# Two heads of a pair in one key tile and one query tile, in the first batch of a decay attention

## The chip, the cores and the metric

The kernel runs on one core of a Trainium2 chip. The metric is the device time of one execution in microseconds (us). A core has TensorE (PE; its weight loads are listed as PEld), VectorE (DVE), ScalarE (ACT), GpSimd (POOL) and SyncE (SP), which issues the DMAs. Each engine works through its own instructions in their order and waits on the others by semaphores.

## The reference

Causal attention with a decay, for 4 batches, 8 heads, 576 tokens and a head dimension of 64, followed by two feed-forward layers over 2304 tokens (width 512, inner width 2048):

```python
scores = scale * np.matmul(q, k.transpose(0, 1, 3, 2))
cum = np.cumsum(np.log(np.clip(f, 0.0001, 1.0)), axis=-1)
scores = np.where(causal, -1e9, scores + cum[..., :, None] - cum[..., None, :])
attn = softmax(scores)                 # over keys
x = (attn @ v), heads side by side     # 2304 x 512
h = x @ w_in;  g = max(h, 0) + alpha * min(h, 0);  x = g @ w_out     # layer 1
h = x @ w2_in; g = h where h >= 1, 0 where h <= -1, else (h + 1)**2 / 4;  out = g @ w2_out   # layer 2
```

All inputs and weights of the layers come as 64-bit words; q, k, v and f are float32 in the kernel.

## The kernel before

Numbers that need more than the short float32 format of TensorE (float32r) are split in two: a high part, which is the value cast to float32r (ScalarE), and a low part, which is the value less its high part (VectorE). A product of two such numbers is then a sum of products of parts.

**Attention.** The loop `for u, pr in head_list()` (line 446) goes over 8 units and 4 pairs of heads in each. A unit is a batch and a range of queries: 0 to 256, or 256 to 576. Units 0 and 1 are batch 0; the code calls them `plain` (line 451). They lie before the phase in which values and probabilities are split too, so their product with the values runs in plain float32 (line 714), while later batches use three float32r products (lines 720 to 722).

For each pair of heads: k and q of both heads are loaded (`load_k`, `load_q`, lines 465 and 469), keys with both heads side by side (128 columns, 64 of each head), queries with room for two copies of each head. `dup_q` (line 478, ScalarE) fills the second copy. TensorE transposes the keys in chunks of at most 512 columns (`ktr`, line 499): rows 0 to 63 of the result are head 0, rows 64 to 127 head 1. From it each head gets a key tile of its own (`khi` and `klo`, lines 512 and 515): the high part in the 64 rows of that head, the low part in the other 64. A head's query tiles (`qtr`, `qhi`, `qlo`, lines 528 to 540) hold the same query twice, over all 128 rows, as high part and as low part. The scores of a block of 128 keys are then two products over 128 rows (`qk`, line 602): key tile with the query's high part, and with its low part:

```python
for t in range(2):
    nc.tensor.matmul(out=sb.t[:, :m], lhsT=kt.t[:, kb * P:(kb + 1) * P],
                     rhs=qt.t[t][:, qo:qo + m], start=(t == 0), stop=(t == 1))
```

A head of unit 0 has 2 blocks (256 and 128 queries), one of unit 1 has 5 (320, 320, 320, 192 and 64). Each block goes from PSUM to SBUF with its bias (ScalarE, line 618), its diagonal part is masked by GpSimd (line 442), VectorE takes the maximum over blocks (lines 637 and 655), GpSimd the maximum over partitions (line 661, `Mb`), VectorE subtracts (line 677), ScalarE takes the exponential (line 680), TensorE multiplies with the values (line 714). Two columns of sums are inverted and spread over the partitions by DMAs (lines 764 to 778), and the result is split into the layer's input (lines 794 and 797).

**Layers.** The 32 pieces of layer 1's weights are converted from 64-bit words while batch 0's attention runs (`convert`, line 816): one ScalarE instruction, four on VectorE (lines 843 to 862), then the high part (line 870) and the low part (line 875). A piece may start once the piece two before it is done. Layer 1 runs over 9 chunks of 256 tokens and 16 slices of the inner width each (`l1_slice`, line 911: `ps_h`, line 922, and `ps_y`, line 961); chunk 0's slice s needs pieces 2s and 2s + 1. All slices are in one fixed order. Layer 2 follows (lines 1097 and 1144).

**Order of the work.** Nothing is emitted in the order of the loops. `Order.emit` (line 113) simulates the engines with durations written in the code (`pe`, `dve`, `act`, lines 257 to 270) and latencies (`LAT`), and at each step gives an engine that is free the ready task of lowest position. Batch 0's attention has positions from -60 to -36, the conversions from -9 up, the slices from about -2 up: attention goes first and conversions fill what is left. Buffers come from rings (line 297): 2 for queries (`q`), 2 for key tiles (`k`), 3 PSUM banks for transposes and scores (`s`), one query load buffer and in batch 0 a second one (`qr`, `qr1`). SP's queue holds all DMAs in the planned order; a load that waits for its buffer holds up what is behind it.

Of the kernel before, what the change touches and what calls it, by code (L numbers as in the profile page):

```python
# [10 lines left out]
F32 = mybir.dt.float32  # L11
# [4 lines left out]
ALU = mybir.AluOpType  # L16
# [84 lines left out]
class Order:  # L101
# [6 lines left out]
    def add(self, eng, dur, fn, pos, deps=(), new=(), use=(), share=1.0, move=0):  # L108
        t = Task(eng, dur, fn, pos, deps, list(new), list(use), share, move)
        self.tasks.append(t)  # L110
        return t
# [81 lines left out]
def kernel(  # L193
# [63 lines left out]
    def pe(n, cnt=1):  # L257
        return cnt * (max(n, 240) / 2.4 + 13)
# [4 lines left out]
    def dve(n, ptr=False):  # L263
        return 68 + n * 1.042 + (60 if ptr else 0)
# [4 lines left out]
    def act(n, bias=False):  # L269
        return 93 + n * 0.833 + (93 if bias else 0)  # L270
# [68 lines left out]

    KC = 4 * P


# [29 lines left out]
    for t in RAW:  # L374
        nc.gpsimd.memset(t[S % P:, NKB - 1], 0.0)
    for t in QR:
        nc.gpsimd.memset(t[S % P:, 2], 0.0)

    first = cpool.tile([P, 2], F32, name="first")
    nc.gpsimd.partition_all_reduce(first, ident[:, :2], P, ReduceOp.max)  # L380
# [1 line left out]
    def load_tok(dst, src, b, pr, t0, t1):  # L382
        n = (t1 - t0) // P
        for j in range(2):
            if n:
                nc.sync.dma_start(
                    out=dst[:, 0:n, j, :],
                    in_=src[b, 2 * pr + j, t0:t0 + n * P, :].rearrange("(c p) d -> p c d", p=P))
        r = t1 - t0 - n * P
        if r:  # L390
            nc.sync.dma_start(
                out=dst[:r, n, :, :],
                in_=src[b, 2 * pr:2 * pr + 2, t0 + n * P:t1, :].rearrange("h p d -> p h d"))
# [52 lines left out]
    for u, pr in head_list():  # L446
# [19 lines left out]
            kb_.t = RAW[kb_.slot]  # L466
            load_tok(kb_.t, k, b, pr, 0, nk)

        def load_q(qb_=qb_, b=b, pr=pr, q0=q0, q1=q1):
            qb_.t = QR[0] if qb_.ring is R["qr"] else ph["qr"]  # L470
            load_tok(qb_.t[:, :, :, 0, :], q, b, pr, q0, q1)

        T["lk"] = add("SP", tok_issue(0, nk), load_k, p0 - 3, [last.get("lv"), last.get("lk")], new=[kb_],
                      move=moved(2 * nk, 256))
# [4 lines left out]
            t = qb_.t[:, :-(-n // P)]  # L479
            nc.scalar.copy(out=t[:, :, :, 1, :], in_=t[:, :, :, 0, :])  # L480

        T["lq"] = add("ACT", act(-(-n // P) * P), dup_q, p0 - 2, [last["lq"]], use=[qb_])


        nsplit = sum(y[2] > PVF for y in blocks)
# [8 lines left out]

        for t0 in range(0, nkp, KC):
            t1 = min(nkp, t0 + KC)
            pb = Buf(R["s"])

            def ktr(pb=pb, kb_=kb_, t0=t0, t1=t1):
                pb.t = ps_a.tile([P, 512], F32, tag=f"s{pb.slot}", name="pst")  # L500
                for c in range(t0 // P, t1 // P):
                    nc.tensor.transpose(
                        pb.t[:, c * P - t0:(c + 1) * P - t0],
                        kb_.t[:, c, :, :].rearrange("p j d -> p (j d)"), ident)

            a = last["ktr"] = add("PE", 112 * (t1 - t0) // P, ktr, p0 - 1, [T["lk"], last.get("ktr")],
                                  new=[pb] + (kx if t0 == 0 else []), use=[kb_] + ([] if t0 == 0 else kx))
            for j in range(2):
                hr = slice(j * D, (j + 1) * D)
                lr = slice(D - j * D, 2 * D - j * D)  # L510

                def khi(j=j, hr=hr, pb=pb, t0=t0, t1=t1, k_of=k_of):
                    nc.scalar.copy(out=k_of(j)[hr, t0:t1], in_=pb.t[hr, :t1 - t0])

                def klo(j=j, hr=hr, lr=lr, pb=pb, t0=t0, t1=t1, k_of=k_of):
                    nc.vector.tensor_tensor(out=k_of(j)[lr, t0:t1], in0=pb.t[hr, :t1 - t0],  # L516
                                            in1=k_of(j)[hr, t0:t1].bitcast(F32), op=ALU.subtract)

                h = add("ACT", act(t1 - t0), khi, p0 - 1, [a], use=[pb, kx[j]])
                kready[j] += [h, add("DVE", dve(t1 - t0), klo, p0 - 1, [h], use=[pb, kx[j]])]  # L520

        qx, qready = [], [[], []]
        for j in range(2):
            pb, qb = Buf(R["s"]), Buf(R["q"])
            qx.append(qb)
            np_ = -(-n // P)

            def qtr(pb=pb, qb_=qb_, j=j, np_=np_):
                pb.t = ps_a.tile([P, 512], F32, tag=f"s{pb.slot}", name="pst")
                for c in range(np_):  # L530
                    nc.tensor.transpose(  # L531
                        pb.t[:, c * P:(c + 1) * P], qb_.t[:, c, j].rearrange("p x d -> p (x d)"), ident)

            def qhi(pb=pb, qb=qb, n=n):
                qb.t = [ap1.tile([P, NMAX], F32R, tag=f"q{x}{qb.slot}", name=f"q{x}") for x in "HL"]
                nc.scalar.copy(out=qb.t[0][:, :n], in_=pb.t[:, :n])

            def qlo(pb=pb, qb=qb, n=n):
                nc.vector.tensor_tensor(out=qb.t[1][:, :n], in0=pb.t[:, :n], in1=qb.t[0][:, :n].bitcast(F32),
                                        op=ALU.subtract)  # L540

            a = add("PE", 112 * np_, qtr, pos_of(2 * pr + j) - 1, [T["lq"], last.get("qtr")], new=[pb], use=[qb_])
            last["qtr"] = a
            h = add("ACT", act(n), qhi, pos_of(2 * pr + j) - 1, [a], new=[qb], use=[pb])
            qready[j] = [h, add("DVE", dve(n), qlo, pos_of(2 * pr + j) - 1, [h], use=[pb, qb])]
# [36 lines left out]
        for j in range(2):  # L582
# [16 lines left out]
            for x, (kb, qo, m, off) in enumerate(blocks):  # L599
                sb = Buf(R["s"])  # L600

                def qk(sb=sb, kb=kb, qo=qo, m=m, kt=kx[j], qt=qx[j]):
                    sb.t = ps_a.tile([P, 512], F32, tag=f"s{sb.slot}", name="ps_s")
                    for t in range(2):
                        nc.tensor.matmul(out=sb.t[:, :m], lhsT=kt.t[:, kb * P:(kb + 1) * P],  # L605
                                         rhs=qt.t[t][:, qo:qo + m], start=(t == 0), stop=(t == 1))

                a = add("PE", pe(m, 2), qk, pb_, kready[j] + qready[j] + [last_qk], new=[sb], use=[qx[j], kx[j]],
                        share=min(1.0, m / 256))
                last_qk = a  # L610
                sbufs.append((sb, a))

                Sb, so, new = S_of[kb]

                def evac(Sb=Sb, sb=sb, m=m, so=so, new=new, bias=nb[:, kb, hd:hd + 1]):
                    if new:
                        Sb.t = ap2.tile([P, GMAX], F32, tag=f"S{Sb.slot}", name="S")
                    nc.scalar.activation(out=Sb.t[:, so:so + m], in_=sb.t[:, :m], func=AF.Identity, bias=bias)  # L618

                e = last["ev"] = add("ACT", act(m, True) - 30, evac, pb_, [a, nb_ready, last.get("ev")], new=[Sb] if new else [],  # L620
                                     use=[sb] + ([] if new else [Sb]))
                base = q0 + qo - kb * P
                w = min(m, P - base)
                if w > 0:
                    e = add("POOL", 300, lambda Sb=Sb, so=so, w=w, base=base: causal(
                        Sb.t[:, so:so + w], base), pb_, [e], use=[Sb])
                ev.append(e)
# [587 lines left out]
```

## Time and profile before

| | us |
|---|---|
| median of 3 runs | 1079.76 (1079.24 to 1083.73) |
| profiled execution, own time | 1081.37 |
| its span, first to last instruction | 1079.6 |
| TensorE busy in the span | 1015.3 |
| VectorE busy | 764.9 |
| ScalarE busy | 665.7 |
| GpSimd busy | 143.5 |

The granted TensorE clock is 0.978 of full speed over the span; it is below 1 only before 180 us. In the trace a line number is that of the instruction in the kernel, an engine is idle before an instruction until its last releaser, and the busy time of an engine is the union of its instructions' durations. On TensorE successive products overlap: the distance of two starts is what a product costs in a row, the duration of one includes its way through the array.

### The profile page before, as it was taken

Reading aid. Unit: us, or ns where it says so; the run is one execution under the profiler, and the core shown is the slowest. Engines: PE = TensorE matmul, PEld = TensorE weight load, DVE = VectorE, ACT = ScalarE, POOL = GpSimd, SP = SyncE. Lnnn points to the kernel's source line nnn. Section 1 sums busy time; section 2 is a strip of 40 time slices with the busy share of each in tenths; the row PEclk is TensorE's granted clock in tenths of the full one; section 3 lists DMA queues with packets and bytes.
Section 4 is the critical chain, followed back from the end, with each engine's and each line's share of the span. In section 5 each row is a group of like instructions: output and inputs, shape, how many; then the busy total and the mean of one; then the engine's idle time right before and its main releaser. Section 6 shows DMA issues by size and latency. Waiting matters only on the chain.

```text
span 1079.6 us, 19362 instructions
## 1 busy us (share of the span) xinstructions
PE 1015.3 (94%) x6549; PEld 925.0 (86%) x6549; DVE 764.9 (71%) x1928; ACT 665.7 (62%) x1754; POOL 143.5 (13%) x244
## 2 busy tenths in 40 slices
PE   3659788999999999999998999999999999999998
PEld 2438678999999999999998999988888888888887
DVE  5989998778777787687773999985455445445443
ACT  5977778978788887888773566553343334333332
POOL 2421224222223222222110000000000000000000
PEclk9868989999999999999999999999999999999999
DMA  7565323312124121232202553531001001000001
GB/s 202 134 173 162 100 48 90 74 38 66 35 45 92 35 62 29 51 86 41 55 7 84 178 157 118 154 100 59 1 12 67 1 1 39 1 1 30 11 1 40
DMA packets 125651, 72.28 MB, mean 67 GB/s; under 512 B 89424, under 2 KB 119120, under 8 KB 125552
## 3 DMA queue, kind: packets, MB, share of 16 engines
q1 hardware_dynamic: 125552, 71.04, 24.5%
q8 instruction: 52, 0.85, 0.4%
q14 instruction: 47, 0.39, 0.1%
HBM read 61.42 MB, written 9.51 MB: 66 GB/s over the span
## 4 chain that ended last, share of the span: by engine, by line
PE 76%; issue 8%; DVE 7%; ACT 5%; POOL 2%; DMA 2%; SPq 0%; POOLq 0%; ACTq 0%; DVEq 0%
PE ps_h L1097 18%; PE ps_z L1144 18%; PE ps_y L961 15%; PE ps_h L922 15%; PE ps_s L605 3%; PE ps_o L714 1%; PE ps_o L722 1%; PE ps_o L720 1%; PE ps_o L721 1%; POOL Mb L661 1%; PE pst L531 1%; DVE S L677 1%; ACT S L680 1%; POOL S L442 1%; DVE kT L516 1%
## 5 line engine op out<-in xcount | busy, mean ns | idle before, releaser
L922 PE MATMUL ps_h<-x,w 128*128 128x256 f32 x1728 | 236.8, 287 | 6.3 <-DVE g L935 5.3
L961 PE MATMUL ps_y<-gH,w 128*128 128x256 f32 x1152 | 236.9, 289 | 0.0
L922 PEld LDWEIGHTS ps_h<-x,w 128*128 128x128 f32 x1728 | 219.4, 192 | 8.8 <-DVE g L935 6.7
L961 PEld LDWEIGHTS ps_y<-gH,w 128*128 128x128 f32 x1152 | 190.8, 193 | 0.3 <-ACT gH L941 0.2
L1097 PE MATMUL ps_h<-xw,w 128*128 128x512 f32 x768 | 184.5, 389 | 0.0
L1144 PE MATMUL ps_z<-w,gH 128*128 128x512 f32 x576 | 177.7, 390 | 0.0
L1097 PEld LDWEIGHTS ps_h<-xw,w 128*128 128x128 f32 x768 | 144.2, 188 | 29.9
L961 PE MATMUL ps_y<-gL,w 128*128 128x256 f32 x576 | 164.3, 285 | 1.0 <-DVE gL L944 0.9
L1122 ACT CAST gH<-g 128x256 fp32r<-128x256 f32 x144 | 58.6, 407 | 161.4 <-PE ps_z L1144 160.7
L1125 DVE TENSOR_TENSOR gL<-g,gH 128x256 fp32r<-128x256 f32 x144 | 61.0, 424 | 125.2 <-ACT gH L1122 125.0
L1144 PEld LDWEIGHTS ps_z<-w,gH 128*128 128x128 f32 x576 | 107.2, 188 | 21.3
L1114 ACT ACTIVATE g<-g,half 128x256 f32<-128x256 f32 x144 | 73.3, 509 | 70.0 <-DVE g L1110 69.8
L961 PEld LDWEIGHTS ps_y<-gL,w 128*128 128x128 f32 x576 | 111.1, 193 | 2.1 <-DVE gL L944 1.9
L1144 PE MATMUL ps_z<-w,gL 128*128 128x512 f32 x288 | 112.1, 389 | 0.0
L618 ACT ACTIVATE S<-ps_s,nb 128x320 f32<-128x320 f32 (+3 forms) x224 | 100.0, 448 | 17.6 <-PE ps_s L605 15.6
L442 POOL TENSOR_SCALAR_AFFINE_SELECT S<-S 128x128 f32<-128x128 f32 (+1 forms) x160 | 62.7, 396 | 338.1 <-ACT S L618 329.0
L605 PE MATMUL ps_s<-qH,kT 128*128 128x320 f32 (+3 forms) x224 | 76.1, 340 | 16.3 <-ACT S L618 7.5
L1117 DVE TENSOR_TENSOR g<-ps_h,g 128x256 f32<-128x256 f32 x144 | 60.9, 423 | 39.9 <-ACT g L1114 39.3
L935 DVE SCALAR_TENSOR_TENSOR g<-g,calpha,ps_h 128x256 f32<-128x256 f32 x144 | 68.6, 477 | 28.8 <-ACT g L932 27.5
L661 POOL PARTITION_ALL_REDUCE Mb<-Mx x64 | 79.0, 1234 | 65.8 <-ACT Mx L645 28.3
L680 ACT ACTIVATE S<-S 128x320 f32<-128x320 f32 (+1 forms) x192 | 79.2, 424 | 10.3 <-DVE S L677 9.5
L932 ACT ACTIVATE g<-ps_h 128x256 f32<-128x256 f32 x144 | 54.9, 381 | 43.6 <-PE ps_h L922 42.7
(85 smaller groups left out, 1651.1 us busy)
## 6 DMA issues: line engine op xcount, KB each, us to landing
raw<-in_moe_w_in_dram SPq DMA_DIRECT2D x32, 512.0 KB
raw<-in_moe_w_out_dram SPq DMA_DIRECT2D x32, 512.0 KB
x<-ysb SPq DMA_DIRECT2D x36, 128.0 KB
x<-x SPq DMA_DIRECT2D x9, 512.0 KB
out_dram<-osb SPq DMA_DIRECT2D x18, 256.0 KB
qr<-in_q_dram SPq DMA_DIRECT2D x64, 64.0 KB
raw<-in_k_dram SPq DMA_DIRECT2D x32, 128.0 KB
raw<-in_v_dram SPq DMA_DIRECT2D x24, 128.0 KB
```

Of the source, the lines that this page charges most:

```text
L442: nc.gpsimd.affine_select(out=sl, in_=sl, pattern=[[1, sl.shape[1]]], compare_op=ALU.is_ge, fill=NEG, base=base, channel_multiplier=-1)
L605: nc.tensor.matmul(out=sb.t[:, :m], lhsT=kt.t[:, kb * P:(kb + 1) * P], rhs=qt.t[t][:, qo:qo + m], start=(t == 0), stop=(t == 1))
L618: nc.scalar.activation(out=Sb.t[:, so:so + m], in_=sb.t[:, :m], func=AF.Identity, bias=bias)
L661: nc.gpsimd.partition_all_reduce(Mb.t[:, :n], Mx.t[:, :n], P, ReduceOp.max)
L680: ex = add("ACT", act(gn), lambda Sb=Sb, gn=gn: nc.scalar.activation(out=Sb.t[:, :gn], in_=Sb.t[:, :gn], func=AF.Exp, scale=-SCALE), pb_, ...
L922: nc.tensor.matmul(out=hb.t, lhsT=a[:, sl], rhs=b, start=(cc == 0 and t == 0), stop=(cc == NCC - 1 and t == 2))
L935: nc.vector.scalar_tensor_tensor(out=gb.t, in0=gb.t, scalar=calpha[:, s:s + 1], in1=hb.t, op0=ALU.mult, op1=ALU.add)
L961: nc.tensor.matmul(out=Y[c][e // 2][:, e % 2, :], lhsT=a[:, sl], rhs=b, start=(s == 0 and t == 0 and e % 2 == 0), stop=(s == NF - 1 and t ...
L1097: nc.tensor.matmul(out=hb.t, lhsT=a[:, sl], rhs=b, start=(cc == 0 and t == 0), stop=(cc == NCC - 1 and t == 2))
L1114: nc.scalar.activation(out=gb.t, in_=gb.t, func=AF.Square, scale=0.5, bias=half)
L1125: nc.vector.tensor_tensor(out=gg.t[1], in0=gb.t, in1=gg.t[0].bitcast(F32), op=ALU.subtract)
L1144: nc.tensor.matmul(out=zb[tg].t, lhsT=a[:, sl], rhs=b, start=(s == 0 and t == 0), stop=(s == NF - 1 and t == 2))
```

## The change

In units 0 and 1 the two heads of a pair stay together in the 128 partitions. There is one high key tile and one low key tile for the pair (`khi2`, `klo2`), and one pair of query tiles (`qtr2`, `qhi2`, `qlo2`), with head 0 in rows 0 to 63 and head 1 in rows 64 to 127. The query is loaded with both heads side by side and not duplicated. A block's scores are three products over the 64 rows of the head: high key with high query, low key with high query, high key with low query. Both key tiles are in use until the second head's scores are done. The clearing of the query load buffers covers the columns from index 1 on. Later batches are as before.

```diff
-        nc.gpsimd.memset(t[S % P:, 2], 0.0)
+        nc.gpsimd.memset(t[S % P:, 1:], 0.0)
...
+            if plain:
+                qb_.t = qb_.t.rearrange("p c j x d -> p (c j x d)")[:, :3 * P].rearrange("p (c j d) -> p c j d", j=2, d=D)
+            load_tok(qb_.t if plain else qb_.t[:, :, :, 0, :], q, b, pr, q0, q1)
...
-        T["lq"] = add("ACT", act(-(-n // P) * P), dup_q, p0 - 2, [last["lq"]], use=[qb_])
+        T["lq"] = last["lq"] if plain else add("ACT", act(-(-n // P) * P), dup_q, p0 - 2, [last["lq"]], use=[qb_])
...
+            if plain:
+                def khi2(pb=pb, t0=t0, t1=t1, k_of=k_of):
+                    nc.scalar.copy(out=k_of(0)[:, t0:t1], in_=pb.t[:, :t1 - t0])
+
+                def klo2(pb=pb, t0=t0, t1=t1, k_of=k_of):
+                    nc.vector.tensor_tensor(out=k_of(1)[:, t0:t1], in0=pb.t[:, :t1 - t0],
+                                            in1=k_of(0)[:, t0:t1].bitcast(F32), op=ALU.subtract)
+
+                h = add("ACT", act(t1 - t0), khi2, p0 - 1, [a], use=[pb, kx[0]])
+                kready[0] += [h, add("DVE", dve(t1 - t0), klo2, p0 - 1, [h], use=[pb, kx[0], kx[1]])]
+                kready[1] = kready[0]
-            for j in range(2):
+            for j in range(0 if plain else 2):
...
+        if plain:
+            pb, qb = Buf(R["s"]), Buf(R["q"])
+            np_ = -(-n // P)
...
+                for c in range(np_):
+                    nc.tensor.transpose(
+                        pb.t[:, c * P:(c + 1) * P], qb_.t[:, c].rearrange("p j d -> p (j d)"), ident)
...
+            a = last["qtr"] = add("PE", 112 * np_, qtr2, p0 - 1, [T["lq"], last.get("qtr")], new=[pb], use=[qb_])
+            h = add("ACT", act(n), qhi2, p0 - 1, [a], new=[qb], use=[pb])
+            qready = [[h, add("DVE", dve(n), qlo2, p0 - 1, [h], use=[pb, qb])]] * 2
+            qx = [qb, qb]
-        for j in range(2):
+        for j in range(0 if plain else 2):
...
+                    if plain:
+                        hr = slice(j * D, (j + 1) * D)
+                        for t, (a, b) in enumerate(((0, 0), (1, 0), (0, 1))):
+                            nc.tensor.matmul(out=sb.t[:, :m], lhsT=kx[a].t[hr, kb * P:(kb + 1) * P],
+                                             rhs=qt.t[b][hr, qo:qo + m], start=(t == 0), stop=(t == 2))
+                        return
...
-                a = add("PE", pe(m, 2), qk, pb_, kready[j] + qready[j] + [last_qk], new=[sb], use=[qx[j], kx[j]],
+                a = add("PE", pe(m, 3 if plain else 2), qk, pb_, kready[j] + qready[j] + [last_qk], new=[sb],
+                        use=[qx[j]] + (kx if plain else [kx[j]]),
```

## Rows read from the trace of the kernel before

**Rows 1.** The page, part 1: engine, busy us, share of the span, instructions.

```profile
span 1079.6 us, 19362 instructions
...
PE 1015.3 (94%) x6549; PEld 925.0 (86%) x6549; DVE 764.9 (71%) x1928; ACT 665.7 (62%) x1754; POOL 143.5 (13%) x244
```

**Rows 2.** Busy time by engine in three stretches; the first line names the columns.

```profile
core 0: us, PE busy (x) PEld busy (x) DVE busy (x) ACT busy (x) POOL busy (x), PEclk, DMA share, GB/s
...
18.60:80.00 61.40, 35.28 (x125) 26.05 (x125) 57.59 (x133) 49.95 (x127) 22.10 (x30) 0.78 0.56 154
80.00:180.00 100.00, 84.70 (x549) 74.33 (x549) 95.78 (x230) 74.87 (x180) 24.46 (x33) 0.92 0.38 101
180.00:300.00 120.00, 118.23 (x954) 116.46 (x954) 96.24 (x264) 102.67 (x304) 30.01 (x54) 1.00 0.25 56
```

**Rows 3.** VectorE's waits from 19 to 180 us: total, times, longest.

```profile
DVE r L785 <- DMA sums<-spread: 2.2, 1, 2.2
DVE Mx L655 <- POOL S L442: 1.5, 8, 0.2
```

**Rows 4.** TensorE's waits from 18.6 to 180 us.

```profile
PE ps_o L714 <- ACT S L680: 11.3, 6, 4.5
PE ps_s L605 <- DVE kT L516: 7.5, 4, 4.6
```

**Rows 5.** Timeline of VectorE: start, duration, line, operation, output and input, count.

```profile
178.96 0.70 DVE L875 TENSOR_TENSOR w<-val,w 128x512 fp32r<-128x512 f32 x1
```

**Rows 6.** VectorE's groups, 0 to 150 us: busy us, mean ns; idle before.

```profile
L516 DVE TENSOR_TENSOR kT<-pst,kT 64x256 fp32r<-64x256 f32 (+2 forms) x24 | 11.2, 466 | 4.0 <-ACT kT L513 3.4
...
L539 DVE TENSOR_TENSOR qL<-pst,qH 128x256 fp32r<-128x256 f32 (+1 forms) x16 | 7.1, 452 | 0.3
```

**Rows 7.** Timeline of VectorE, 10 to 24 us, the first pair.

```profile
10.70 0.86 DVE L516 TENSOR_TENSOR kT<-pst,kT 64x256 fp32r<-64x256 f32 x2 [3.44 <-ACT kT L513]
11.59 0.76 DVE L539 TENSOR_TENSOR qL<-pst,qH 128x256 fp32r<-128x256 f32 x2
...
18.61 0.35 DVE L637 TENSOR_TENSOR Mx<-S 128x128 f32<-128x128 f32 x1 [3.37 <-POOL S L442]
```

**Rows 8.** Timeline of VectorE, 156 us.

```profile
156.83 0.41 DVE L539 TENSOR_TENSOR qL<-pst,qH 128x256 fp32r<-128x256 f32 x1
157.17 0.68 DVE L875 TENSOR_TENSOR w<-raw,w 128x512 fp32r<-128x512 f32 x1
```

**Rows 9.** Timeline of GpSimd, 0 to 20 us.

```profile
9.72 0.34 POOL L375 MEMSET raw<- 64x128 f32 x2
10.00 0.56 POOL L377 MEMSET qr<- 64x256 f32 x2
17.70 0.37 POOL L380 PARTITION_ALL_REDUCE first<-ident  x1 [7.14 <-issue]
```

**Rows 10.** ScalarE's groups by line, 0 to 150 us.

```profile
L513 ACT CAST kT<-pst 64x256 fp32r<-64x256 f32 (+2 forms) x24 | 9.6, 401 | 3.7 <-PE pst L502 3.5
L536 ACT CAST qH<-pst 128x256 fp32r<-128x256 f32 (+1 forms) x17 | 6.4, 391 | 0.1
...
L480 ACT COPY qr<-qr 128x256 f32<-128x256 f32 (+1 forms) x9 | 4.0, 450 | 0.7 <-DMA qr<-in_q_dram 0.7
```

**Rows 11.** Timeline of TensorE, 149 to 151 us.

```profile
149.80 0.31 PE L605 MATMUL ps_s<-qH,kT 128*128 128x320 f32 x1
149.95 0.31 PE L605 MATMUL ps_s<-qL,kT 128*128 128x320 f32 x1
```

**Rows 12.** The score products (line 605) alone, 80 to 160 us: PE busy.

```profile
80.00:160.00 80.00, 15.79 (x60) 10.22 (x60) 0.92 0.40 107
```

**Rows 13.** Timeline of TensorE, 9.5 to 20 us.

```profile
11.70 0.71 PE L413 MATMUL pst<-ident,cum 32*128 32x32 f32 x5 [0.96 <-DVE kT L516]
12.34 0.58 PE L605 MATMUL ps_s<-qH,kT 128*128 128x256 f32 x1
...
13.52 0.55 PE L605 MATMUL ps_s<-qH,kT 128*128 128x256 f32 x1
```

More of the change, by code (lines that the diff above doesn't have):

```diff
@@ L467, in load_k, with load_q @@
             load_tok(kb_.t, k, b, pr, 0, nk)
-        def load_q(qb_=qb_, b=b, pr=pr, q0=q0, q1=q1):
+        def load_q(qb_=qb_, b=b, pr=pr, q0=q0, q1=q1, plain=plain):
             qb_.t = QR[0] if qb_.ring is R["qr"] else ph["qr"]
-            load_tok(qb_.t[:, :, :, 0, :], q, b, pr, q0, q1)
+            if plain:
+                qb_.t = qb_.t.rearrange("p c j x d -> p (c j x d)")[:, :3 * P].rearrange("p (c j d) -> p c j d", j=2, d=D)
+            load_tok(qb_.t if plain else qb_.t[:, :, :, 0, :], q, b, pr, q0, q1)
         T["lk"] = add("SP", tok_issue(0, nk), load_k, p0 - 3, [last.get("lv"), last.get("lk")], new=[kb_],
@@ L522, with qtr2, qhi2, qlo2 @@
         qx, qready = [], [[], []]
-        for j in range(2):
+        if plain:
+            pb, qb = Buf(R["s"]), Buf(R["q"])
+            np_ = -(-n // P)
+            def qtr2(pb=pb, qb_=qb_, np_=np_):
+                pb.t = ps_a.tile([P, 512], F32, tag=f"s{pb.slot}", name="pst")
+                for c in range(np_):
+                    nc.tensor.transpose(
+                        pb.t[:, c * P:(c + 1) * P], qb_.t[:, c].rearrange("p j d -> p (j d)"), ident)
+            def qhi2(pb=pb, qb=qb, n=n):
+                qb.t = [ap1.tile([P, NMAX], F32R, tag=f"q{x}{qb.slot}", name=f"q{x}") for x in "HL"]
+                nc.scalar.copy(out=qb.t[0][:, :n], in_=pb.t[:, :n])
+            def qlo2(pb=pb, qb=qb, n=n):
+                nc.vector.tensor_tensor(out=qb.t[1][:, :n], in0=pb.t[:, :n], in1=qb.t[0][:, :n].bitcast(F32),
+                                        op=ALU.subtract)
+            a = last["qtr"] = add("PE", 112 * np_, qtr2, p0 - 1, [T["lq"], last.get("qtr")], new=[pb], use=[qb_])
[3 more added lines that the diff above has]
+        for j in range(0 if plain else 2):
             pb, qb = Buf(R["s"]), Buf(R["q"])
@@ L600, with qk @@
                 sb = Buf(R["s"])
-                def qk(sb=sb, kb=kb, qo=qo, m=m, kt=kx[j], qt=qx[j]):
+                def qk(sb=sb, kb=kb, qo=qo, m=m, kt=kx[j], qt=qx[j], kx=kx, j=j, plain=plain):
                     sb.t = ps_a.tile([P, 512], F32, tag=f"s{sb.slot}", name="ps_s")
+                    if plain:
[4 more added lines that the diff above has]
+                        return
                     for t in range(2):
```

## The prediction

> **What bounds the kernel now.** I read the page's shares first. TensorE is busy 94% of the span and VectorE 71% [rows 1], which looks like a kernel bound by TensorE; but a share is a mean over stages, so I cut the span into stretches [rows 2]. From 180 to 300 us TensorE is busy 118.23 of 120 us, and after that much the same. From 18.6 to 180 us it is not: 35.28 + 84.70 = 120.0 busy in 161.4 us, so 41.4 us idle, while VectorE is busy 57.59 + 95.78 = 153.4 of the same 161.4 us, 95%. Nearly all of the first batch's attention lies in this stretch. The waits say the same: from 19 us on VectorE's longest waits are 2.2 us for a DMA and 1.5 us in eight pieces for GpSimd [rows 3], while TensorE waits 11.3 us for exponentials and 7.5 us for the key tile's low part, made by VectorE [rows 4].
>
> What VectorE does there is of two kinds: attention of batch 0, which the planner prefers, and the conversion of the first layer's 32 weight pieces, which fills every gap. The last conversion starts at 178.96 us [rows 5]; the sixteen slices of token chunk 0 need the pieces one after the other, and only behind them can TensorE run without a break. So the end of the kernel is, to first order, the time at which VectorE has done the conversions and the batch-0 work before them, plus a fixed stretch of TensorE work. A microsecond of VectorE work removed between 18.6 and 180 us moves the end by about as much, if nothing takes VectorE's place.
>
> **The change part by part.**
>
> *VectorE, removed.* In batch 0 a pair made, for each key chunk, two low parts of 64 rows; now one of 128 rows. It made two query low parts; now one. Before 150 us stand 24 key instructions, 11.2 us together, and 16 query instructions, 7.1 us [rows 6]. All are of batch 0 (8 pairs: 4 with one key chunk, 4 with two). Half of each goes: 5.6 + 3.55 = 9.15 us. The duration goes by columns and not by rows, by the first pair: two 64x256 key instructions take 0.86 us and two 128x256 query instructions 0.76 us [rows 7]. So the one that stays costs what one of the two cost.
>
> Not all of 9.15 us is path. Back to back a query instruction of 128x256 holds VectorE for 0.34 us (156.83 to 157.17), not its recorded 0.41 [rows 8]: 8 instructions less by 0.07 make 0.55 us of the gain void. And the first pair's share, 0.86/2 + 0.76/2 = 0.81 us, lies before VectorE's idle of 3.37 us that ends at 18.61 us with GpSimd's first causal select [rows 7]; what is saved ahead of that idle makes it longer. That leaves 9.15 - 0.55 - 0.81 = 7.8 us. The key instructions I count whole: each stands behind its own ScalarE cast and the two do not overlap (0.86 us for two).
>
> *GpSimd, added.* The clearing of the query tiles covers twice the columns, 2 x 256 to 2 x 512. Two clears of 64x128 take 0.34 us, two of 64x256 0.56 us [rows 9], so 128 columns more cost two of them 0.22 us, and 256 more an estimated 0.44 us. They stand directly ahead of the instruction that shows 7.14 us of idle and ends with the reduction at 17.70 us [rows 9], behind which GpSimd's first causal selects queue and behind those VectorE. If that idle counts from the end of the clears, all 0.44 us reach the path; if it counts from elsewhere, nothing. I take the whole, 0.4 us.
>
> *ScalarE, removed.* Half of 24 key casts (9.6 us), half of 16 of the query casts (about 6.0 of the 6.4 us in the group of 17) and the 8 batch-0 duplications of the query (of 9 in the group, about 3.6 of 4.0 us) [rows 10]: 4.8 + 3.0 + 3.6 = 11.4 us. ScalarE is busy 49.95 + 74.87 of 161.4 us [rows 2] and ends none of VectorE's long waits, so I count it as nothing directly. At best it takes part of VectorE's remaining 8.0 us of idle away.
>
> *TensorE, added and removed.* A head of the first unit has 2 score blocks, one of the second 5: 7 x 8 = 56 blocks, each with a third product, so 56 products more, with their weight loads. 20 query transposes go (4 x 2 + 4 x 3). The trace shows no product over 64 rows. Above: it costs a full one, 0.15 us for 320 columns at the full granted clock (149.80 to 149.95) [rows 11], and I estimate 0.13 as a mean over blocks of 64 to 320 columns. Between 80 and 160 us stand 60 score products, the 30 blocks of the last three pairs [rows 12]: 30 x 0.13 = 3.9 us, less 9 transposes at an estimated 0.11: 2.9 us. Below: nothing, if half a tile went in half the time. I take the full one, since the nearest row is one of the same columns. In 80 to 180 us TensorE has 15.3 us idle [rows 2], so the 2.9 us are covered by waits; but four fifths of the stretch are busy, the idle isn't where one would like it, and I charge a quarter, 0.7 us. Before 80 us there are 26.1 us idle for the other 26 blocks (at the lower clock level, 1.2 GHz, twice 0.13 each, 6.8 us), charged nothing. If this cover is gone, both are paid: 2.9 + 6.8 = 9.7 us.
>
> *Changing between 64 and 128 rows.* 56 blocks are entered and left, 112 changes. The nearest row is the one place where the trace goes from products of 32 rows (the transposes of the decay, 11.70 us) to products of 128: the next scores product, 128x256, shows 0.58 us, and the same form 1.2 us later, with no such change ahead of it, 0.55 us [rows 13]. So a change costs 0.03 us there, 112 x 0.03 = 3.4 us at most, in idle: nothing charged. The upper bound is the pipeline emptied each time: a single 128x320 product shows 0.31 us where the next begins after 0.15 [rows 11], so 0.16 us a change.
>
> The Trainium skill speaks against the change here: TensorEngine Tiling (Array Packing), section Key Properties, says that a change of tiling mode drains TensorE. The trace's one change, 0.03 us beside 0.16 for an emptied pipeline, doesn't bear this out as a visible price, but it is one place at a low load; by the rule all 112 changes would pay the larger price, which is the third rival.
>
> *Queues, order, buffers.* The query's DMAs are as many and as large as before; on SP's queue their loads waited for ScalarE's duplication or the second head's transposes and now wait for one batch of transposes, which comes earlier: nothing or a little gained. The second head's query now comes with the first head's, in the same instructions, so nothing that stands between the two is delayed by it. Both key tiles are now held until the second head's scores are done; the next pair's transposes needed both before, so no new wait. The planner re-sorts all engines by its own durations; this can cost or give a few microseconds and has no sign I can read off.
>
> *Sum.* 7.8 - 0.4 - 0.7 = 6.7 us off. The profiled execution's own time is 1081.37 us (span 1079.6 and 1.8 around it), so it would be 1074.7; it lies 1.6 us over the median of the runs, 1079.76, and from that I forecast 1079.76 - 6.7 = 1073.1 us.
>
> **The rivals.**
>
> *First: faster than forecast.* Here VectorE's 8.0 us of idle shrink too, because ScalarE has 11.4 us less and the second head of a pair is ready earlier. For it: ScalarE feeds every VectorE step. Against: VectorE's listed waits are for DMA and GpSimd [rows 3]. If half of it went, the end would come 4 us earlier still, 1069.
>
> *Second: no change.* TensorE takes VectorE's place from 80 to 180 us. It is busy 84.70 of 100 us there already; the three pairs' share of the gain, by columns of keys and queries 7.8 x (3 x 960) / (4 x 960 + 3 x 512) = 4.2 us, is asked from it while 2.9 us of work are added. If its idle is all latency that can't be filled, that half of the gain is lost and the 2.9 us are paid; 7.8 - 4.2 = 3.6 us of the gain before 80 us stay, less the 0.4 of the clears and the 2.9: 0.3 us off, 1079.5. For it: TensorE's waits there end with exponentials, whose chain through GpSimd the change leaves alone. Against: the chain holds only attention, and it is conversions that end last.
>
> *Third: slower.* Each change of row count empties TensorE at 0.16 us. From 80 us on that is 30 x 2 x 0.16 = 9.6 us, with 2.9 for the products 12.5 of the 15.3 us idle; before 80 us 52 x 0.16 to 0.32 = 8.3 to 16.6 us more in 26.1 us idle. If none can be filled, 20.8 to 29.1 us would be added against 7.4 gained; with half of it hidden, about 3 to 7 us slower, 1083 to 1087. It decides above about 0.07 us a change if no idle takes it up, (7.4 - 2.9) / 60, and above 0.2 if all does, (15.3 - 2.9) / 60. For it: the blocks lie scattered among 128-row work. Against: the 0.03 us of [rows 13].
>
> That the change doesn't do what it says (a 128-row VectorE instruction slower than a 64-row one) is contradicted by [rows 7]; it would end with the second.
>
> **How the numbers follow.** Forecast 0.55, first rival 0.10, second 0.22 (with the void change), third 0.13. A measurement of this kernel can tell about 0.5%, 5.4 us, from no change; the line lies at 1074.4, near the forecast, and the planner's re-sorting moves the forecast by some 3 us either way. Of the forecast's 0.55 I put 0.45 beyond the line and 0.10 within; the first rival is beyond it, the second within, of the third 0.11 beyond 1085.2 and 0.02 within. Faster 0.55, same 0.34, slower 0.11. The range, 1066 to 1083, takes in the first and second rival and the third's beginning; the forecast's own is 1070 to 1077.
>
> **What would show it.** Right: the last conversion starts at about 172 us instead of 178.96; VectorE's key and query groups of batch 0 halve to 5.6 and 3.6 us; TensorE's idle before 180 us falls by more than the added products; from there to the end the stretch is as long as before. Wrong: score products whose first one starts late behind a product of the other row count (third rival); TensorE near 95% busy between 80 and 170 us with VectorE below 92% (second); the last conversion earlier by over 9 us (first). The forecast falls if the end of the conversions and the end of the kernel move by different amounts.

## The result, and the profile after

The changed kernel takes 1089.89 us (median of 6 runs, 1087.82 to 1090.13) beside 1081.22 us (6 runs, 1079.24 to 1083.73) of the kernel before on the same chip: ratio 1.0077, 95% interval 1.0062 to 1.0093, 8.7 us slower. The forecast was 1073.1 us, range 1066 to 1083: it had the wrong sign. The profiled execution has a span of 1088.2 us.

The page's shares and the same three stretches as in [rows 2] (columns there):

```profile
span 1088.2 us, 19370 instructions
...
PE 1038.4 (95%) x6585; PEld 936.3 (86%) x6585; DVE 759.7 (70%) x1908; ACT 655.0 (60%) x1726; POOL 139.0 (13%) x244
```

```profile
18.60:80.00 61.40, 43.64 (x135) 30.66 (x136) 53.56 (x123) 42.46 (x107) 20.52 (x32) 1.00 0.58 155
80.00:180.00 100.00, 92.22 (x526) 75.11 (x525) 89.89 (x211) 68.73 (x162) 20.32 (x30) 0.86 0.34 98
180.00:300.00 120.00, 117.87 (x952) 115.81 (x951) 94.53 (x260) 100.65 (x296) 29.65 (x55) 1.00 0.24 54
```

VectorE's busy time between 18.6 and 180 us fell from 57.59 + 95.78 to 53.56 + 89.89 us, in part because work moved behind 180 us: over the whole span it fell by 5.2 us. But TensorE is busy 23.1 us longer in the whole span (1038.4 for 1015.3), with 36 instructions more. Cutting both kernels at 180 us shows how that reaches the end (first fence before, second after; first two columns: the stretch and TensorE's busy time with its instructions):

```profile
0.00:180.00 180.00, 125.57 (x697) 104.58 (x697) 159.87 (x377) 132.14 (x321) 49.52 (x80) 0.88 0.48 131
180.00:1100.00 920.00, 889.76 (x5854) 820.43 (x5853) 605.07 (x1552) 533.54 (x1434) 93.99 (x164) 1.00 0.20 53
```

```profile
0.00:180.00 180.00, 141.33 (x684) 109.74 (x685) 149.07 (x345) 117.04 (x280) 43.31 (x76) 0.92 0.47 130
180.00:1100.00 920.00, 897.04 (x5903) 826.56 (x5901) 610.62 (x1565) 537.96 (x1446) 95.65 (x169) 1.00 0.19 53
```

Behind 180 us TensorE is almost never idle (9.8 us before, 11.2 after, the rest of the span less the busy time), so the end is that time plus the work still left. Up to 180 us TensorE worked 15.8 us longer and yet did 13 instructions fewer: 15.8 us of its 54.4 us of idle time were filled with longer work, not with more of it. 897.04 - 889.76 = 7.3 us more of work were left, and with 1.3 us more idle that is the 8.6 us by which the span grew. This sum, TensorE's busy time and idle time on either side of 180 us, is used for every run below.

On VectorE the groups of [rows 6] halved as the prediction said, to 5.4 and 3.6 us:

```profile
L516 DVE TENSOR_TENSOR kT<-pst,kT 128x256 fp32r<-128x256 f32 (+2 forms) x12 | 5.4, 458 | 3.6 <-ACT kT L513 3.6
L552 DVE TENSOR_TENSOR qL<-pst,qH 128x256 fp32r<-128x256 f32 (+1 forms) x8 | 3.6, 448 | 0.0
```

But its timeline shows the wait for the first causal select grown from 3.37 us ([rows 7]) to 7.10, and the last conversion at 183.28 us, where [rows 5] has 178.96 and the forecast about 172:

```profile
21.31 0.35 DVE L680 TENSOR_TENSOR Mx<-S 128x128 f32<-128x128 f32 x1 [7.10 <-POOL S L443]
...
183.28 1.09 DVE L918 TENSOR_TENSOR w<-val,w 128x512 fp32r<-128x512 f32 x1
```

GpSimd's timeline, for [rows 9], shows where that comes from in this execution: the query clears take 0.43 us longer, as estimated, but the reduction behind them starts 2.7 us later, because the idle time ahead of it is longer as well:

```profile
10.16 0.99 POOL L378 MEMSET qr<- 64x512 f32 x2
20.39 0.37 POOL L381 PARTITION_ALL_REDUCE first<-ident  x1 [9.25 <-issue]
```

And this is where TensorE's time went. Its timeline at 102 us, a block of scores (two columns of numbers: start, duration; 64*128 marks products over 64 rows):

```profile
101.86 0.70 PE L757 MATMUL ps_o<-S,vF 128*128 128x320 f32 x2
102.48 0.46 PE L643 MATMUL ps_s<-qH,kT 64*128 64x192 f32 x2
102.79 0.27 PE L643 MATMUL ps_s<-qL,kT 64*128 64x192 f32 x1
102.99 0.81 PE L757 MATMUL ps_o<-S,vF 128*128 128x320 f32 x2
103.39 0.52 PE L1004 MATMUL ps_y<-gH,w 128*128 128x256 f32 x1
```

At the same place the kernel before has, with no change of rows:

```profile
102.37 0.70 PE L714 MATMUL ps_o<-S,vF 128*128 128x320 f32 x2
102.66 0.49 PE L605 MATMUL ps_s<-qH,kT 128*128 128x192 f32 x1
102.99 0.27 PE L605 MATMUL ps_s<-qL,kT 128*128 128x192 f32 x1
103.11 0.51 PE L714 MATMUL ps_o<-S,vF 128*128 128x192 f32 x2
```

The product at 102.66 starts early but is held itself (0.49 us for the 0.27 of the like one behind it), so starts are compared over the whole passage. Going in: two value products and one of scores take 0.62 us before the change (102.37 to 102.99); after it two value products and two of scores take 0.93 (101.86 to 102.79). One score product of this width takes 0.12 (102.99 to 103.11), so 0.93 - 0.62 - 0.12 = 0.19 us are the price. Coming out: the last score product takes 0.20 us to the next start for 0.12, and the value pair behind it 0.40 (102.99 to 103.39) for 0.29 (102.37 to 102.66), together 0.19 us. So this block paid about 0.38 us, with no idle time recorded: it counts as busy.

### The profile page after: what moved, and what is told of

Its sections match the earlier page's. It is cut to its first block, busy times and chain, and to the rows that moved or that the text cites. A ratio compares the mean times of both kernels' runs of the same rounds, so it can differ in the third digit from the quotient of the medians.

```text
span 1088.2 us, 19370 instructions
## 1 busy us (share of the span) xinstructions
PE 1038.4 (95%) x6585; PEld 936.3 (86%) x6585; DVE 759.7 (70%) x1908; ACT 655.0 (60%) x1726; POOL 139.0 (13%) x244
## 4 chain that ended last, share of the span: by engine, by line
PE 82%; DVE 5%; ACT 4%; issue 4%; DMA 4%; SPq 1%; POOL 0%; ACTq 0%; POOLq 0%; DVEq 0%
PE ps_h L1140 18%; PE ps_z L1187 18%; PE ps_h L965 17%; PE ps_y L1004 16%; PE ps_s L647 3%; PE ps_o L757 3%; PE ps_s L643 1%; DMA sums<-spread 1%; PE ps_o L763 1%; PE ps_o L765 1%; PE ps_o L764 1%; PE pst L567 1%; PE pst L505 1%; DMA raw<-in_k_dram 1%; DMA raw<-in_moe_w_out_dram 1%
## 5 line engine op out<-in xcount | busy, mean ns | idle before, releaser
L443 POOL TENSOR_SCALAR_AFFINE_SELECT S<-S 128x128 f32<-128x128 f32 (+1 forms) x160 | 57.7, 365 | 359.7 <-ACT S L661 349.0
L757 PE MATMUL ps_o<-S,vF 128*128 128x64 f32 (+4 forms) x256 | 75.0, 388 | 11.2 <-ACT S L723 5.6
```

The source lines that it names most:

```text
L757: nc.tensor.matmul(out=o, lhsT=vf, rhs=Sb.t[:, off - g0:off - g0 + m], start=(kb == 0), stop=last)
```

## Experiments

All edits are of the changed kernel unless the text says "the kernel before". Ratios are to the kernel before, with 95% intervals.

**What do the 64 rows cost? (e1, e2.)** Only the rows of the score products are changed back to 128 here; order, number of products and everything else are those of the changed kernel.

```
-                        hr = slice(j * D, (j + 1) * D)
+                        hr = slice(0, P)
```

> The changed kernel, with the three score products of batch 0 over all 128 rows instead of the 64 of one head (the scores are then a sum over both heads; the instruction order on every engine is the same). Theory M, changes between 64-row and 128-row products empty TensorE: in the changed kernel a 64-row block following another product starts some 0.3 us late and what follows it some 0.1 us late, 56 blocks, 20 to 25 us of TensorE time; without them TensorE is no longer full at 100 to 120 and 160 to 180 us, and the kernel takes 1081 to 1086 us. Theory O, the re-sorted order of the engines is at fault: no change, 1088 to 1091 us. Theory S, the late start of GpSimd: no change either.

Measured: 1081.63 us, 1.0006 (0.9995 to 1.0017). The two kernels' ratios differ by 0.71%, 7.7 us: almost all of the loss. TensorE's busy time falls back to that of before (1015.2 us), and the work left at 180 us to below it:

```profile
0.00:180.00 180.00, 128.98 (x765) 110.99 (x766) 156.94 (x369) 125.58 (x310) 51.84 (x86) 0.89 0.48 133
180.00:1100.00 920.00, 886.24 (x5822) 815.32 (x5821) 600.89 (x1539) 528.79 (x1418) 91.60 (x158) 1.00 0.19 53
```

The conversions now end at 171.94 us, the 172 of the forecast; the end of the kernel did not move with them. In e2 the third product is left out and the 64 rows stay:

```
-   for t, (a, b) in enumerate(((0, 0), (1, 0), (0, 1))):
+   for t, (a, b) in enumerate(((0, 0), (1, 0))):
```

> The changed kernel without the third score product (high key with low query is left out of batch 0's scores), 64 rows kept and the order the same. Theory P, the 56 added products are what costs: 56 x 0.13 to 0.27 us = 7 to 15 us less TensorE time and 1081 to 1086 us. Theory M: the emptying stays and the product of 0.13 us behind it is a small part, 1086 to 1089 us.

Measured: 1087.08 us, 1.0052 (1.0038 to 1.0065), 2.7 us better than the changed kernel by the ratios. The third products are a small part.

**What do the clears cost? (e3, e4, e7.)** GpSimd clears what it cleared before; the one chunk more is cleared by VectorE.

```
-        nc.gpsimd.memset(t[S % P:, 1:], 0.0)
+        nc.gpsimd.memset(t[S % P:, 1], 0.0)
+    nc.vector.memset(QR[0][S % P:, 2], 0.0)
```

> The changed kernel with GpSimd clearing as many columns as before (two of 64x256; the third part that later batches need is cleared by VectorE). Theory S: GpSimd's first reduction comes at 17.7 us again instead of 20.4, VectorE's idle ahead of the first maximum falls from 7.1 to about 4.4 us, and the kernel takes 1086 to 1088 us. Rival: the reduction's start hangs on the code load and the transfers beside it, not on the clears; it comes at 20 us still (0.4 us earlier at most), and the time is 1089 to 1090 us.

Measured: 1086.37 us, 1.0047 (1.0034 to 1.0061), 3.2 us better; the reduction starts at 17.55 us. e4 has this edit and that of e1:

> Both edits: products over 128 rows (scores a sum over both heads) and the clears as before. If M and S both hold and add up, 1078 to 1084 us; if only M holds, the same as with 128 rows alone; if neither, 1089 us.

Measured: 1079.37 us, 0.9982 (0.9972 to 0.9992), 2.6 us better than e1. This is the change without its two added costs, and it gives 1.9 us where the forecast had 7.8 for VectorE alone. e7 is the kernel before with the 64-row clears of key and query tiles (lines 375 and 377) moved to VectorE:

> The kernel before with the clears of the key and query load buffers on VectorE instead of GpSimd, nothing else. Theory S, the reduction's code load starts when the clears are done: it comes about 0.8 us earlier than 17.7 us and the kernel is 0.5 to 2 us faster than before, 1078.5 to 1080. Rival, the code load ends when the transfers beside it let it: 17.5 us or later and no change.

Measured: 1077.45 us, 0.9969 (0.9958 to 0.9980), 3.4 us better; the reduction starts at 15.95 us. So in three pairs of kernels clears ahead of the first reduction cost 2.6 to 3.4 us (0.43 us of clears in two pairs, 0.90 us in e7). How is not settled: the idle time ahead of the reduction (6.3 to 9.4 us over these profiles, released by nothing the trace shows) was 8.5 us in e5 below although its clears are the small ones, and 8.2 and 8.5 us in g1 and g3, whose clears are those of the kernel before (7.1).

**Two products of 128 rows (e5).** e4 with e2's edit:

> The changed kernel with products over 128 rows (a sum over both heads), only two of the three (high key with low query left out) and the clears as before: of the change only VectorE's, ScalarE's and the transposes' savings are left, in the changed kernel's order. Theory D, a microsecond of VectorE ahead of the last conversion is one of the end: 1073 to 1076 us, 4 to 7 us under the kernel before. Theory T, TensorE itself is full from 140 us on, so that conversions ready 8 us earlier find it behind: no better than with three products, 1078 to 1080 us.

Measured: 1079.59 us, 0.9988 (0.9978 to 0.9997), no better than e4 with three. The third product over 128 rows is free here.

**Does the order hide the price? (e8.)** e3, with the planner told what a block costs:

```
-   a = add("PE", pe(m, 3 if plain else 2), qk, ...
+   a = add("PE", pe(m, 3) + 450 if plain else pe(m, 2), qk, ...
```

> The changed kernel, correct, clears as before, and the planner told 450 ns more for each block of 64-row products. Theory O, the order that the planner finds without knowing the price adds to the loss: 1080 to 1084 us. Theory M alone: the price is paid whatever the order, 1085 to 1088 us, as with the clears alone (1086.4).

Measured: 1079.93 us, 0.9986 (0.9976 to 0.9996), 6.6 us better than e3 although the same products run and their blocks stand in more groups between other work, 47 for 41 (counted in the timelines): TensorE's busy time is 1033.8 us for e3's 1036.1. What falls in the two profiles is the idle time behind 180 us (11.7 to 8.9) and the work left there (892.3 to 890.1).

**Both heads' blocks together (e6).** Each block's six products of the two heads are issued in turns, rows 0 to 63 and 64 to 127, into two PSUM tiles, so that there are fewer changes (25 groups for 41); the planner is told the price, as above. The edit does more: all clears go to VectorE, as in e7, each head's blocks leave PSUM in an order of their own, and the queries' transposes wait for the keys'.

```
+   for t, (a, b) in enumerate(((0, 0), (1, 0), (0, 1))):
+       for j, sb in enumerate(two):
+           hr = slice(j * D, (j + 1) * D)
+           nc.tensor.matmul(out=sb.t[:, :m], lhsT=kx[a].t[hr, kb * P:(kb + 1) * P], ...
```

> The changed kernel, correct, with the blocks of both heads of a pair taken together: six products over 64 rows, alternating between rows 0 to 63 and rows 64 to 127, so 28 stretches of 64-row work instead of 56; clears on VectorE; the planner is told 450 more per stretch. Theory M: half the entries and exits, half the price, 10 to 12 us of TensorE time saved, and the late start gone: 1079 to 1084 us. If besides products on different rows run side by side (starts a few ns apart in the trace), 1076 to 1080 us. Rival: it is the 64-row products themselves that are slow, so nothing but the late start changes, 1086 us.

Measured: 1072.93 us, 0.9929 (0.9913 to 0.9945): faster than both kernels. That it meets the time forecast for the change as it stood says nothing for the forecast's steps. How much of it each part of the edit gives was not taken apart. TensorE's busy time is 1012.6 us, less than before the change. Its timeline at 106 us:

```profile
105.90 0.33 PE L777 MATMUL ps_o<-S,vF 128*128 128x64 f32 x2
106.15 0.56 PE L626 MATMUL ps_s<-qH,kT 64*128 64x320 f32 x4
106.55 0.31 PE L626 MATMUL ps_s<-qL,kT 64*128 64x320 f32 x2
106.79 0.38 PE L1024 MATMUL ps_y<-gH,w 128*128 128x256 f32 x1
```

Six products of 320 columns leave in 0.64 us (106.15 to 106.79), the changes at both ends included: 0.107 each, where [rows 11] has 0.15 for one over 128 rows. The last two together last 0.31 us, as long as one alone in [rows 11]: products over the two halves of the rows ran side by side.

**Does TensorE wait for values? (e9, e10, e11.)** In the changed kernel TensorE once waits 5.6 us for the values' DMA, a wait that isn't among the longest before. A second value buffer for every other pair of the first unit lets that load go earlier: e9 on e4, e10 on e3, e11 on e6.

> As the kernel with products over 128 rows and the clears as before (scores a sum over both heads; 1079.4 us, first slice of the layer at 85.2 us), with a second value buffer for the odd pairs of the first unit, so that a value load doesn't wait for the pair before. Theory F, the end is the time of the first layer slice (82.6 us before) plus a stretch of TensorE work (990 us here, 997 before): without the 7.3 us that TensorE waits for the values the first slice comes at 78 to 82 us and the kernel takes 1072 to 1077 us. Theory D, VectorE's work is the bound: no change, 1079.

> The changed kernel, correct, with the clears as before (1086.4 us) and the second value buffer for the first unit. Theory F: the first slice moves from 89.8 to 83 to 87 us and the kernel takes 1080 to 1084 us. Theory M alone (TensorE's time in 64-row work): 1085 to 1087 us.

> The kernel with both heads' blocks taken together (1072.9 us; first slice at 81.4 us; TensorE waits only 1.5 us for values there) with the second value buffer for the first unit. Theory F: little to take away, first slice 79 to 82 us, 1070 to 1074 us.

Measured: e9 1081.79 us, 1.0000 (0.9987 to 1.0012); e10 1091.84 us, 1.0099 (1.0079 to 1.0119); e11 1072.01 us, 0.9916 (0.9902 to 0.9931). The wait went, and TensorE's idle time before 180 us fell from 36.2 us in e3 to 31.9 in e10. But e10 came out slower: it has 4.1 us more busy time, and behind 300 us TensorE waits 5.2 us for the input of a later slice, where e3 (second fence) waits 1.8. Columns: us in total, times, longest.

```profile
PE ps_h L969 <- ACT x L840: 5.2, 1, 5.2
```

```profile
PE ps_h L966 <- ACT x L838: 1.8, 1, 1.8
```

The theory that the values held the end falls. A wait taken away here came back as another in the new order.

**Is VectorE the bound at all? (e12, e13, e14.)** The kernel before, with VectorE's conversion work cut. e12 leaves out the clamp (line 843), in the conversions of both layers and not of the first alone; e13 keeps two VectorE operations of five in the first layer's conversions; e14 is e13 without ScalarE's first operation as well.

> The kernel before without the first of VectorE's four bit operations in each weight conversion (the clamp of tiny and huge values is left out), which takes 32 x 0.41 = 13 us of VectorE work out of the first layer's conversions and nothing else. Theory D: 10 to 13 us faster, 1068 to 1071 us. Theory F: conversions come earlier but the first slice does not; 0 to 5 us faster, 1076 to 1081 us.

> The kernel before, with the first layer's 32 conversions cut to two VectorE operations of five (clamp, shift and the joining of the top word are left out, so the weights of the first layer are wrong): 32 x (0.47 + 0.45 + 0.70) = 52 us of VectorE work less before 180 us. If VectorE's throughput sets the end, as the prediction's step has it: most of TensorE's 54 us of idle time before 180 us can go, of which some 40 us lie behind the first 20 us; at 0.55 us of end for each us of VectorE the end comes 20 us or more earlier. If the idle time hangs on each block's own chain through ScalarE and VectorE: under 6 us.

> The same, and the first layer's 30 conversions that are done in place lose ScalarE's first operation too (30 x 0.675 = 20 us of ScalarE less; the weights of the first layer are wrong). If ScalarE is the engine that held the end while VectorE had room: another 10 us or more earlier than the run beside it. If neither engine's throughput sets TensorE's idle time: within 4 us of it.

Measured: e12 1082.15 us, 1.0014 (1.0003 to 1.0026); e13 1059.17 us, 0.9809 (0.9788 to 0.9831); e14 1063.26 us, 0.9840 (0.9820 to 0.9861). The stretches of e12 and of e13:

```profile
0.00:180.00 180.00, 128.60 (x731) 107.52 (x731) 157.49 (x364) 137.68 (x349) 50.57 (x88) 0.88 0.49 135
180.00:1100.00 920.00, 887.44 (x5819) 817.03 (x5819) 588.62 (x1501) 527.78 (x1407) 89.85 (x156) 1.00 0.19 52
```

```profile
0.00:180.00 180.00, 141.47 (x880) 122.77 (x880) 140.83 (x348) 154.09 (x410) 53.75 (x100) 0.91 0.51 145
180.00:1100.00 920.00, 868.60 (x5672) 798.87 (x5670) 582.93 (x1484) 507.56 (x1345) 81.96 (x144) 1.00 0.18 50
```

In e13 VectorE's busy time over the span is 41.1 us less (723.8 for 764.9; the expected 52 us are durations, which overlap), and the end comes 21 us (1.9%) earlier, 0.5 us for each. In e12 it is 18.8 us less, with half of the 64 clamps in the first layer, and that brings nothing, though the conversions then end at 166.8 us. e14 has less work than e13 and is 3.4 us slower, with intervals that just overlap: less ScalarE work gave nothing. That the new order is what cost the 3.4 us is not shown. Even in e13, with VectorE idle for 39 us before 180 us, TensorE is idle for 38.5 us there, of 54.4 before.

**The price of a change by itself (g1, g2, g3).** In the kernel before, six more products of 256 columns stand ahead of each of the second layer's 64 wide slices, where TensorE has no idle time and the granted clock reads 1.00. Over all rows (g1), over rows 0 to 63 (g2), by turns (g3, shown):

```
+   if w == 2:
+       xh = xb.t[:, 0, 0, :]
+       nc.tensor.matmul(out=hb.t[:, :C1], lhsT=wh[0:64, :P], rhs=xh[0:64, :C1], start=True, stop=True)
+       nc.tensor.matmul(out=hb.t[:, :C1], lhsT=wh[0:P, :P], rhs=xh[0:P, :C1], start=True, stop=True)
...
```

> The kernel before, with six more products of 256 columns over all 128 rows ahead of each of the 64 wide slices of the second layer (724 to 1064 us, where TensorE has no idle time); their results are overwritten, so the output is the reference's. The base for the two runs beside it. All theories: 64 x 6 x 0.107 to 0.12 us (256 columns at 2.4 GHz, the pitch of the 256-column products of the first layer) = 41 to 46 us, 1122 to 1127 us.

> The same six products, all over rows 0 to 63: each slice enters and leaves the 64-row form once. If a block's price is that read in the trace of the changed kernel (0.33 us on entering, 0.11 us on leaving): 64 x 0.44 = 28 us above the run with 128 rows. If changes are nearly free and most of the 23 us of TensorE time came from the lower granted clock: within 6 us of it. If each 64-row product is dearer by itself (its weights not loaded ahead, 0.05 us or more): 64 x 6 x 0.05 = 19 us and more above, and then the mixed run costs half of that at most for its products.

> The same six products, by turns over 64 and over 128 rows: each slice enters and leaves the 64-row form three times. Price by the change, 0.44 us for entering and leaving: 64 x 3 x 0.44 = 84 us above the run with 128 rows, three times the run with 64 rows alone. Price by the product: half of that run's excess. Changes nearly free (0.03 us as in the rows before the prediction): within 12 us of the run with 128 rows, and the 23 us of the changed kernel are then the clock's.

Measured: 1128.92, 1152.28 and 1204.27 us, ratios 1.0440, 1.0659 and 1.1134, each within 0.0031. g3 less g1 is 75.4 us for 64 x 3 times in and out: 0.39 us each (0.37 to 0.42 by the intervals). g2 less g1 is 23.4 us for 64 times: 0.37 us (0.29 to 0.44), so six 64-row products in a row cost what six full ones do, and the price is the change's alone. (The 0.44 us of the expectations count 0.33 us for going in, from the early start at 102.66 above; over the whole passage it is 0.38.) The timelines of g1, g2 and g3 at one slice:

```profile
800.69 0.28 PE L1095 MATMUL ps_h<-xw,w 128*128 128x256 f32 x1
800.80 0.28 PE L1096 MATMUL ps_h<-xw,w 128*128 128x256 f32 x1
800.92 0.28 PE L1097 MATMUL ps_h<-xw,w 128*128 128x256 f32 x1
```

```profile
803.33 0.39 PE L1152 MATMUL ps_z<-w,gL 128*128 128x512 f32 x1
803.65 0.38 PE L1095 MATMUL ps_h<-xw,w 64*128 64x256 f32 x1
803.87 0.28 PE L1096 MATMUL ps_h<-xw,w 64*128 64x256 f32 x1
803.99 0.28 PE L1097 MATMUL ps_h<-xw,w 64*128 64x256 f32 x1
```

```profile
799.97 0.38 PE L1095 MATMUL ps_h<-xw,w 64*128 64x256 f32 x1
800.28 0.38 PE L1096 MATMUL ps_h<-xw,w 128*128 128x256 f32 x1
800.60 0.38 PE L1097 MATMUL ps_h<-xw,w 64*128 64x256 f32 x1
800.90 0.39 PE L1098 MATMUL ps_h<-xw,w 128*128 128x256 f32 x1
```

From start to start a product takes 0.12 us among its like and 0.31 where the rows change: 0.19 us a change, in either direction. The weight loads tell how. This is g2's view of them (PEld), the last load of 128 rows and the first two of 64:

```profile
803.11 0.19 PEld L1152 LDWEIGHTS ps_z<-w,gL 128*128 128x128 f32 x1
803.64 0.18 PEld L1095 LDWEIGHTS ps_h<-xw,w 64*128 64x128 f32 x1 [0.35 <-issue]
803.75 0.19 PEld L1096 LDWEIGHTS ps_h<-xw,w 64*128 64x128 f32 x1
```

The load at 803.11 lies 0.22 us ahead of its product at 803.33, beneath the product before; the one at 803.64 starts with its own (0.01 us ahead by these rows). Across a change the next weights aren't loaded early.

## Why the prediction was wrong

**The changes of row count: the step that turned the sign.** The prediction charged nothing for 112 changes, from 0.03 us in [rows 13], with 0.16 us as the upper bound. The price is 0.19 us where TensorE is never idle (g1 to g3), and changing the rows alone brought 7.7 us back (e1). The row was misread: [rows 13] compares two products' own durations, while the cost lies in the starts, and the second of the two is no undisturbed product, since its weight load follows 0.22 us of idle time. The trace of before did show a price at its one place. From 12.34 us to the next start are 0.38 us, from there to the one after, over the same 256 columns, 0.22: 0.16 us late, at the lower clock level (256 columns last 0.41 us here, 0.28 in g1). The product of 13.52, out of its wait, takes 0.35 (first fence TensorE, second its weight loads):

```profile
12.72 0.41 PE L605 MATMUL ps_s<-qL,kT 128*128 128x256 f32 x1
12.94 0.31 PE L605 MATMUL ps_s<-qH,kT 128*128 128x128 f32 x1
...
13.87 0.42 PE L605 MATMUL ps_s<-qL,kT 128*128 128x256 f32 x1
```

```profile
13.49 0.29 PEld L605 LDWEIGHTS ps_s<-qH,kT 128*128 128x128 f32 x1 [0.22 <-issue]
```

The third rival had mechanism, place and nearly the size; its 1083 to 1087 lies 3 us short of what came, and it had a chance of 0.13. The Trainium skill (TensorEngine Tiling (Array Packing), Key Properties) spoke of a drain at each change of tiling mode; the runs agree that each change is paid, at 0.39 us in and out.

**What TensorE's 23 us more consist of is not shown in full.** In the order of the changed kernel the 56 blocks stand in 41 groups with other work between them (counted in its timeline), so 82 changes and not 112: an estimated 41 x 0.39 = 16 us. Beside that its clock was lower for longer. Before 180 us TensorE was busy at the lower level, 1.2 GHz, for 73.4 us in the changed kernel, 47.6 in the kernel before and 39.6 in e1. This counts the stretches with a granted clock of 0.50 and the one ahead of the first recorded change of the clock (to 79.8, 38.9 and 28.9 us), where products last as long as at 0.50. A product of 320 columns lasts 0.47 us there for 0.31, so a third of the 25.8 us more, an estimated 9 us, may be the clock's. With the 16 us and the third products that is more than 23, so one of these shares is smaller. e1 shows that both go when the rows go back to 128 in the same order.

**The cover was taken for granted.** TensorE's idle time up to 180 us did take up about two thirds: it fell by 15.8 us while 23.1 were added. The third that was not hidden, 7.3 us, is most of the loss. The third rival reckoned with half of it hidden.

**"A microsecond of VectorE work removed moves the end by about as much": false.** The own test of the prediction decided it: the end of the conversions and the end of the kernel had to move together. In e4 the conversions end 8.6 us earlier (170.32 us) and the kernel 1.9; in e12, 12 us earlier and the kernel not at all; in e13, 51 us earlier (127.59 us) and the kernel 21. The rate over a large cut is 0.5 (e13). VectorE at 95% was the busiest engine of the stretch, but most of TensorE's idle time up to 180 us stays when VectorE has room (38.5 of 54.4 us in e13). So 7.8 us on the account were worth 1.9 (e4) to 3.9 (at e13's rate).

**The clears: 0.44 us of work as estimated, 2.6 to 3.2 us of time.** The two cases were "all 0.44 us, or nothing"; that they would cost more than their own time was not among them.

**The order "has no sign I can read off".** It had a size: 6.6 us between e3 and e8, which differ only in what the planner is told of a block. Fewer changes are not the reason, since e8 has more groups than e3. TensorE was busy at the lower clock level for 59.8 us in e8 and 70.7 in e3, counted as above; what else its order does better was not taken apart.

**What held.** VectorE's two groups halved as worked out, but its busy time in all fell by 5.2 us (7.1 in e1), less than the 8.6 that the prediction's terms leave (9.15 - 0.55). ScalarE's fell by 10.7 us for 11.4. The third product costs little (0 to 2.7 us; 0.7 were charged). The account by runs: changes +7.7, clears +2.6, all else -1.9: 8.4 us, beside 8.3 by the ratio.

**Open:** what sets TensorE's idle time before 180 us when VectorE does not; how its 23 us divide between the changes, the clock and the third products; how the clears cost what they cost, and why the idle time ahead of the first reduction varies.

## What to carry to other kernels

Before TensorE is made to work on fewer rows, count how often its row count will change in the issued order, and price a change in a stretch where TensorE is never idle. Read it from start to start, over a passage that ends behind the change and not at the first start after it. If the half-height form is wanted, group all blocks of that form, alternate the two halves, and tell the planner the price: the same arithmetic went from 0.8% slower to 0.7% faster (e6, with the clears moved too). A busy share of 95% doesn't yet make an engine's work worth its time at the end: cut a large piece of it and see.

## What the runs showed that was not expected

Of products over the two row halves, issued by turns, two of 320 columns last as long together as one over 128 rows, 0.31 us, and six leave in 0.64 us with the changes at both ends (e6).

In the changed kernel the granted clock reads 1.00 throughout 20 to 80 us, though its 320-column products last 0.47 us there, as e1's do where the column reads 0.73 (40 to 60 us), and 0.31 in [rows 11]; by that it ran at the lower of its two levels, 1.2 GHz:

```profile
53.45 0.47 PE L643 MATMUL ps_s<-qL,kT 64*128 64x320 f32 x1
```

The same holds for the kernel before up to 38.9 us, where 256 columns last 0.41 us (12.72 above). The column is no proof of full speed by itself; a product's duration is the check.
